# The normaliser's mean as two one-pass products of the squares' halves, split on VectorE

## Chip, cores, metric

One core of a Trainium2 chip. The metric is the device time of one execution in us; the kernel before and each other kernel are run in turns on the same chip, and a ratio is the mean time of one kernel's fast runs over the mean of the other's of the same rounds, so not quite the ratio of the medians that are quoted. The sets of runs were made on different chips, so times of two sets can be compared only roughly: the median of the kernel before lay between 1119.8 and 1122.7 us from set to set. One profiled execution of each kernel gives its trace; a span in a trace is some 2 us shorter than the time of the same execution.

## The reference

```python
def attention(q, k, v, g_norm):            # q, k, v: 8 batches x 8 heads x 576 x 64
    kv  = einsum('bhsd,bhse->bhde', k, v)
    out = einsum('bhsd,bhde->bhse', q, kv)
    rms = sqrt(mean(out * out, axis=-1, keepdims=True) + 1e-06)     # over the 64 of a head
    return out / rms * g_norm

def ffn(x, w_in, w_out):                   # x: 4608 x 512, w_in: 512 x 2048, w_out: 2048 x 512
    h = x @ w_in
    return (h * erf(softplus(h))) @ w_out
```

x is the attention's result, the heads side by side. The weights arrive as 64-bit floats, which the kernel decodes on the chip.

## The kernel before

Work goes by groups of 512 tokens, feature by token: batches 0 to 7, and a ninth group of the 64 tokens left over of each. For a pair of heads the mean over 64 features is a product with a matrix of 1/64, which also spreads the sum over the 64 partitions. Everything is fp32.

```python
def apply():                                   # the output of two heads, and its square
    nc.tensor.matmul(o_ps, lhsT=bd, rhs=qT[:, 0:G], start=True, stop=True)
    ...
    nc.scalar.activation(qT[:, 0:G], o_ps, AF.Square)

def norm():
    ms_ps, u = bank("ms_ps"), st.pop("qT")[:, 0:G]
    nc.tensor.matmul(ms_ps, lhsT=mean_w, rhs=u, start=True, stop=True)      # the mean, 128x512
    nc.scalar.activation(r, ms_ps, AF.Ln, bias=eps_col)                     # r = ms ** -0.5
    nc.scalar.activation(r, r, AF.Exp, scale=-0.5)
    nc.scalar.activation(u, r, AF.Square)
    ... three VectorE steps: one Newton step, times g, into xT ...
```

While one batch goes through the two big products, the attention of the next is done in pieces between them. Batch 0's feed-forward runs in 16 steps of 128 hidden features, beside the decoding of the weights and batch 1's attention:

```python
pieces = attention_pieces(1)               # products, apply, norm for each pair of heads
for n in range(FC):                        # 16 steps
    if n - LAG + 1 >= 0:
        gated(hs[n - LAG + 1], ss[n - LAG + 1])    # VectorE, waits for ScalarE's erf
    if n % BATCH < 3:
        next(pieces)()
    weights(2)                             # join two decoded blocks, split two more
    ... 4 matmuls into h_ps; ScalarE: copy, softplus, every 4th step erf of four units ...
```

From batch 1 on, the two products go block by block with seven multiplications in place of eight (`p_ps` and the sums `a_sums`, `x_sums`, `w_sums`). The first such batch begins with `sums_a`, `sums_x(1)`, then four late gates, then the copy that frees TensorE's bank (one of the buffers that its products go to) for the first product on `x_sums`. From there on a period is one quarter of a batch: 7 + 7 block products and one pair of heads.

Of the kernel before, what the change touches and what calls it, by code (L numbers as in the profile page):

```python
# [37 lines left out]

FP32 = mybir.dt.float32
I32 = mybir.dt.int32  # L40
U32 = mybir.dt.uint32
AF = mybir.ActivationFunctionType
ALU = mybir.AluOpType
# [5 lines left out]
BATCH = 4  # L49
# [4 lines left out]
def kernel(  # L54
# [10 lines left out]
    nc = tc.nc  # L65
    P = 128
    B, H, S, D = q.shape
    DM, DF = moe_w_in.shape[0], moe_w_in.shape[1] // 2
    J = 4
    G = J * P  # L70
    R = S - G
# [8 lines left out]
    const = ctx.enter_context(tc.tile_pool(name="const", bufs=1))  # L80
# [5 lines left out]
    room = ctx.enter_context(ExitStack())  # L86
    early = room.enter_context(tc.tile_pool(name="early", bufs=2))
# [42 lines left out]
    for i in range(2):  # L130
        nc.sync.dma_start(
            out=g_col[i * D : i * D + D, :], in_=g_norm.rearrange("(d one) -> d one", one=1)
# [4 lines left out]

    ident = const.tile([P, P], FP32, name="ident")
    make_identity(nc, ident)
    mean_w = const.tile([P, P], FP32, name="mean_w")  # L140
    nc.vector.memset(mean_w, 0.0)
    for i in range(2):
        nc.vector.memset(mean_w[i * D : i * D + D, i * D : i * D + D], 1.0 / D)
    exp_col = const.tile([P, 1], FP32, name="exp_col")
    nc.vector.memset(exp_col, -896.0 * (1 << 23))
    eps_col = const.tile([P, 1], FP32, name="eps_col")
# [22 lines left out]
    def w_split(which, f):  # L169

        hi = w_raw[which, f].rearrange("p (n two) -> p n two", two=2)[:, :, 1]
        e = early.tile([P, G], I32, name="w_e", tag="w_e", bufs=3)
        m = early.tile([P, G], I32, name="w_m", tag="w_m", bufs=3)
        nc.vector.tensor_scalar(  # L174
            out=e,
            in0=hi,
            scalar1=20,
            scalar2=0x7FF,
            op0=ALU.logical_shift_right,
            op1=ALU.bitwise_and,  # L180
        )
        nc.vector.tensor_scalar(  # L182
            out=e, in0=e, scalar1=896.0, scalar2=1151.0, op0=ALU.max, op1=ALU.min
        )
        nc.scalar.activation(e, e, AF.Identity, scale=float(1 << 23), bias=exp_col)  # L185
        nc.vector.tensor_scalar(  # L186
            out=m,
            in0=hi,
            scalar1=0xFFFFF,
            scalar2=0x100000,  # L190
            op0=ALU.bitwise_and,
            op1=ALU.bitwise_or,
        )
        nc.gpsimd.tensor_scalar(
            out=m.bitcast(FP32), in0=m, scalar1=2.0**-20, scalar2=None, op0=ALU.mult
        )
        w_cv[which, f] = e, m
# [44 lines left out]
    def attention(T, p, pools=None):  # L242

        st = {}
        bd = bd_kv[:, (T * NP + p) % 2, :]

        q_tail, o_tail = slice(P, P + R), slice(P + R, P + 2 * R)
        sb, bufs = (early, 3) if T == 0 else (attp, 1)

        def bank(name):  # L250
            pool, tag = (pools or {}).get(name, (ps_at, "at"))
            return pool.tile([P, G], FP32, name=name, tag=tag)

        def products():
            kv_ps = st["kv"] = bank("kv_ps")
            ks, vs, qs = (x.pop((T, p)) for x in (k_sb, v_sb, q_sb))
            for c in range(C):
                nc.tensor.matmul(  # L258
                    kv_ps[:, 0:P], lhsT=ks[:, c], rhs=vs[:, c], start=(c == 0), stop=(c == C - 1)
                )  # L260
            nc.tensor.transpose(kv_ps[:, q_tail], qs[0:R, J], ident[0:R, 0:R])
            qT = st["qT"] = sb.tile([P, G + R], FP32, name="qT", tag="qT", bufs=bufs)
            for i in range(2):
                s = slice(i * D, i * D + D)
                nc.vector.tensor_copy(out=bd[s, s], in_=kv_ps[s, s])
            nc.vector.tensor_copy(out=qT[:, G:], in_=kv_ps[:, q_tail])
            qt_ps = bank("qt_ps")
            for j in range(J):
                nc.tensor.transpose(qt_ps[:, j * P : j * P + P], qs[:, j], ident)  # L269
            nc.scalar.copy(qT[:, 0:G], qt_ps)  # L270

        def apply():
            qT, o_ps, kv_ps = st["qT"], bank("se_ps"), st.pop("kv")
            nc.tensor.matmul(kv_ps[:, o_tail], lhsT=bd, rhs=qT[:, G:], start=True, stop=True)
            nc.tensor.matmul(o_ps, lhsT=bd, rhs=qT[:, 0:G], start=True, stop=True)  # L275
            nc.vector.tensor_copy(out=x_last[:, p, T * R : T * R + R], in_=kv_ps[:, o_tail])
            st["o"] = o_ps
            nc.scalar.activation(qT[:, 0:G], o_ps, AF.Square)  # L278

        def square():  # L280
            st["o"] = x_last[:, p, :]
            st["qT"] = sb.tile([P, G + R], FP32, name="qT", tag="qT", bufs=bufs)
            nc.scalar.activation(st["qT"][:, 0:G], st["o"], AF.Square)

        def norm():
            ms_ps, u = bank("ms_ps"), st.pop("qT")[:, 0:G]
            nc.tensor.matmul(ms_ps, lhsT=mean_w, rhs=u, start=True, stop=True)  # L287
            r = sb.tile([P, G], FP32, name="rms_r", tag="rms_r", bufs=bufs)
            if T > 0:
                exp_ln_table()  # L290
            nc.scalar.activation(r, ms_ps, AF.Ln, bias=eps_col)
            nc.scalar.activation(r, r, AF.Exp, scale=-0.5)
            nc.scalar.activation(u, r, AF.Square)  # L293
            if T > 0 or p == NP - 1:
                softplus_table()
            nc.vector.scalar_tensor_tensor(  # L296
                out=u, in0=ms_ps, scalar=EPS, in1=u, op0=ALU.add, op1=ALU.mult
            )
            nc.vector.scalar_tensor_tensor(
                out=u, in0=u, scalar=3.0, in1=r, op0=ALU.subtract, op1=ALU.mult  # L300
            )
            if T not in xT:
                xT[T] = xp.tile([P, KC, G], FP32, name="xT", tag="xT")
            nc.vector.scalar_tensor_tensor(
                out=xT[T][:, p, :],
                in0=st.pop("o"),
                scalar=gm_col,
                in1=u,
                op0=ALU.mult,
                op1=ALU.mult,  # L310
            )

        return (products, apply, norm) if T < B else (lambda: None, square, norm)

    def attention_pieces(T):


        for p in range(NP):
            products, apply, norm = attention(T, p)

            def first(products=products, p=p):
                products()
                load_pair(T * NP + p + 2)

            yield from (first, apply, norm)


    NB = FC // BATCH
# [28 lines left out]
    def softplus(h):  # L357
        s = unit("s_sb")
        nc.scalar.activation(s, h, AF.Softplus)  # L359
        return s  # L360
# [22 lines left out]
        for p in range(NP)  # L383
    ]
    for i in range(NP + 2):
        for stage, p in enumerate((i, i - 1, i - 2)):
            if 0 <= p < NP:
                first[p][stage]()
                if stage == 0:
                    if p == 0:  # L390
                        load_pair(3)
                    elif p < 3:
                        load_pair(p + 3)
        if i >= 2:
            weights(1)


    pieces = attention_pieces(1)
    hs, ss = {}, {}
    for n in range(FC):  # L400
        if n - LAG + 1 >= 0:
            gated(hs[n - LAG + 1], ss[n - LAG + 1])

        if n % BATCH < 3:
            next(pieces)()
        weights(2)
        h_ps = ps_h.tile([P, G], FP32, name="h_ps", tag="h")
        for c in range(KC):
            nc.tensor.matmul(  # L409
                h_ps,  # L410
                lhsT=w_in_sb[:, c, n * P : n * P + P],
                rhs=xT[0][:, c, :],
                start=(c == 0),
                stop=(c == KC - 1),
            )
        h = hs[n] = unit("h_sb")
        nc.scalar.copy(h, h_ps)  # L417
        ss[n] = softplus(h)
        if n % BATCH == BATCH - 1:
            erfs([ss[i] for i in range(n - BATCH + 1, n + 1)])  # L420
        if n - LAG >= 0:
            project(n - LAG, hs[n - LAG])

    room.close()
    late = room.enter_context(tc.tile_pool(name="late", bufs=1))
    acc = room.enter_context(tc.tile_pool(name="acc", bufs=6))
    a_sums = late.tile([P, NB, 3, 2, 2 * P], FP32, name="a_sums")
    w_sums = late.tile([P, NB, 3, 2, H], FP32, name="w_sums")

# [131 lines left out]
    def batch(m, before, seconds, slots):  # L561


        T, b = divmod(m, NB)
# [6 lines left out]
        def piece():  # L571
            if todo:
                todo.pop(0)()

        def second():
            for _ in range(next(places)):
                seconds.pop(0)()
# [19 lines left out]
        add(c22, c21, p5)  # L597
        add(c12, c12, p5)
        e22 = softplus(c22)
        second()  # L600
        piece()
        add(c21, c21, product(a22, t4))
# [21 lines left out]
    for m in range(NB, NG * NB):  # L624
        T, b = divmod(m, NB)
# [46 lines left out]
```

## Time and profile before

| | value | read from |
|---|---|---|
| time | 1121.2 us (1119.7 to 1121.7) | 3 runs |
| TensorE busy, 300 us to 900 us | 100%, clock 1.00 | busy time by stage |
| period of that part | 28.26 us in 22 of the 27 intervals between 28 means (the first is 29.93, the last four 25.1 to 25.8) | starts of the means |
| one mean, start to the next product | 0.86 us | timeline |
| VectorE busy, 50 us to 200 us | 76 to 83% | busy time by stage |
| four steps of batch 0's feed-forward | 42.1 us | starts of the gates (VectorE's h times erf) that wait for erf |

How to read it: a timeline line gives start, length, engine, source line, operation, destination and sources, and in square brackets the idle time before it with what ended it. Lengths of matmuls overlap, so prices are taken from one start to the next. The prediction below shows the lines.

### The profile page before, as it was taken

Reading aid. Unit: us, or ns where it says so; the run is one execution under the profiler, and the core shown is the slowest. Engines: PE = TensorE matmul, PEld = TensorE weight load, DVE = VectorE, ACT = ScalarE, POOL = GpSimd, SP = SyncE. Lnnn points to the kernel's source line nnn. Section 1 sums busy time; section 2 is a strip of 40 time slices with the busy share of each in tenths; the row PEclk is TensorE's granted clock in tenths of the full one; section 3 lists DMA queues with packets and bytes.
Section 4 is the critical chain, followed back from the end, with each engine's and each line's share of the span. In section 5 each row is a group of like instructions: output and inputs, shape, how many; then the busy total and the mean of one; then the engine's idle time right before and its main releaser. Section 6 shows DMA issues by size and latency. Waiting matters only on the chain.

```text
span 1121.4 us, 11926 instructions
## 1 busy us (share of the span) xinstructions
PE 1050.5 (94%) x4584; PEld 836.8 (75%) x4584; DVE 713.6 (64%) x1180; ACT 486.5 (43%) x652; POOL 100.7 (9%) x71
## 2 busy tenths in 40 slices
PE   6576887899999999999999999999999999999996
PEld 4232443458888888888888888888888888888885
DVE  1678788637776656675567556755675567666545
ACT  1444444544444444444444444444444455442222
POOL 0257556200000000000000000000000000000000
PEclk9886988999999999999999999999999999999999
DMA  8345434102111211121112111211120001001001
GB/s 206 97 123 146 125 94 127 32 10 61 32 32 32 70 33 32 32 70 32 32 32 70 32 32 32 70 32 33 32 70 1 1 1 38 1 1 38 1 1 38
DMA packets 134488, 55.30 MB, mean 49 GB/s; under 512 B 115488, under 2 KB 131872, under 8 KB 134432
## 3 DMA queue, kind: packets, MB, share of 16 engines
q1 hardware_dynamic: 134432, 54.55, 18.5%
q8 instruction: 36, 0.59, 0.2%
q14 instruction: 20, 0.16, 0.0%
HBM read 45.09 MB, written 9.44 MB: 49 GB/s over the span
## 4 chain that ended last, share of the span: by engine, by line
PE 82%; DVE 10%; ACT 4%; issue 2%; SPq 1%; POOL 0%; DMA 0%; DVEq 0%; ACTq 0%; POOLq 0%
PE p_ps L483 68%; PE kv_ps L258 3%; PE o_ps L336 3%; PE se_ps L275 2%; DVE w_m L207 2%; PE ms_ps L287 2%; DVE e L431 1%; PE qt_ps L269 1%; DVE w_e L203 1%; DVE w_e L182 1%; PE h_ps L409 1%; DVE w_e L174 1%; SPq L121 1%; DVE w_m L186 1%; ACT w_e L185 1%
## 5 line engine op out<-in xcount | busy, mean ns | idle before, releaser
L359 ACT ACTIVATE s_sb<-h_sb 128x512 f32<-128x512 f32 x144 | 89.9, 630 | 337.5 <-DVE h_sb L431 337.0
L431 DVE TENSOR_TENSOR h_sb<-h_sb,p_ps 128x512 f32<-128x512 f32 x224 | 148.2, 684 | 116.0 <-PE p_ps L483 114.8
L483 PE MATMUL p_ps<-w_out_sb,h_sb 128*128 128x256 f32 x768 | 176.4, 380 | 1.0 <-DVE h_sb L585 1.0
L483 PEld LDWEIGHTS p_ps<-w_out_sb,h_sb 128*128 128x128 f32 x768 | 145.8, 190 | 21.5 <-DVE h_sb L585 1.8
L483 PE MATMUL p_ps<-x_sums,a_sums 128*128 128x256 f32 x512 | 122.8, 384 | 4.9 <-issue 4.9
L431 DVE TENSOR_TENSOR e<-e,p_ps 128x512 f32<-128x512 f32 x120 | 80.8, 684 | 71.6 <-PE p_ps L483 71.0
L483 PE MATMUL p_ps<-x_sums,w_in_sb 128*128 128x256 f32 x512 | 121.0, 379 | 0.0
L483 PEld LDWEIGHTS p_ps<-x_sums,a_sums 128*128 128x128 f32 x512 | 98.4, 192 | 28.9 <-issue 16.2
L483 PE MATMUL p_ps<-w_sums,s_sb 128*128 128x256 f32 x512 | 116.3, 380 | 0.0
L483 PEld LDWEIGHTS p_ps<-x_sums,w_in_sb 128*128 128x128 f32 x512 | 97.4, 190 | 25.1 <-issue 13.4
L483 PEld LDWEIGHTS p_ps<-w_sums,s_sb 128*128 128x128 f32 x512 | 95.2, 190 | 15.9 <-DVE h_sb L431 4.0
L483 PE MATMUL p_ps<-xT,w_in_sb 128*128 128x256 f32 x448 | 101.3, 379 | 0.0
L483 PEld LDWEIGHTS p_ps<-xT,w_in_sb 128*128 128x128 f32 x448 | 83.3, 190 | 10.3
L98 ACT ACT_TABLE_LOAD x69 | 88.5, 1283 | 1.2
L431 DVE TENSOR_TENSOR h_sb<-h_sb,s_sb 128x512 f32<-128x512 f32 x128 | 82.2, 685 | 5.5 <-ACT s_sb L364 5.5
L296 DVE SCALAR_TENSOR_TENSOR qT<-ms_ps,qT 128x512 f32<-128x512 f32 x36 | 24.9, 692 | 95.5 <-ACT qT L293 95.5
L409 PE MATMUL h_ps<-xT,w_in_sb 128*128 128x512 f32 x128 | 67.2, 672 | 16.4 <-ACT h_sb L417 11.0
L364 ACT ACTIVATE s_sb<-s_sb 128x512 f32<-128x512 f32 x144 | 78.8, 618 | 0.4
L278 ACT ACTIVATE qT<-se_ps 128x512 f32<-128x512 f32 x32 | 19.0, 594 | 115.5 <-PE se_ps L275 115.5
L409 PEld LDWEIGHTS h_ps<-xT,w_in_sb 128*128 128x128 f32 x128 | 27.8, 221 | 53.6 <-issue 32.6
L258 PEld LDWEIGHTS kv_ps<-v_sb,k_sb 96*128 96x128 f32 x384 | 51.8, 206 | 16.4 <-issue 12.8
L185 ACT ACTIVATE w_e<-w_e,exp_col 128x512 int32<-128x512 int32 x32 | 23.1, 722 | 89.5 <-DVE w_e L182 89.5
(76 smaller groups left out, 1374.7 us busy)
## 6 DMA issues: line engine op xcount, KB each, us to landing
k_sb<-in_k_dram SPq DMA_DIRECT2D x64, 144.0 KB, 3.0
v_sb<-in_v_dram SPq DMA_DIRECT2D x64, 144.0 KB, 3.1
q_sb<-in_q_dram SPq DMA_DIRECT2D x64, 128.0 KB, 2.9
w_raw<-in_moe_w_in_dram SPq DMA_DIRECT2D x16, 512.0 KB, 3.7
w_raw<-in_moe_w_out_dram SPq DMA_DIRECT2D x16, 512.0 KB, 3.8
out_dram<-e SPq DMA_DIRECT2D x28, 256.0 KB, 2.1
q_sb<-in_q_dram SPq DMA_DIRECT2D x32, 32.0 KB, 2.5
out_dram<-o_sb SPq DMA_DIRECT2D x4, 256.0 KB, 2.2
```

Source lines behind the costliest of these rows:

```text
L98: nc.scalar.preload_act_table_set("softplus")
L185: nc.scalar.activation(e, e, AF.Identity, scale=float(1 << 23), bias=exp_col)
L207: nc.vector.scalar_tensor_tensor(out=m, in0=lo, scalar=2.0**-52, in1=m, op0=ALU.mult, op1=ALU.add)
L258: nc.tensor.matmul(kv_ps[:, 0:P], lhsT=ks[:, c], rhs=vs[:, c], start=(c == 0), stop=(c == C - 1))
L275: nc.tensor.matmul(o_ps, lhsT=bd, rhs=qT[:, 0:G], start=True, stop=True)
L296: nc.vector.scalar_tensor_tensor(out=u, in0=ms_ps, scalar=EPS, in1=u, op0=ALU.add, op1=ALU.mult)
L336: nc.tensor.matmul(o_ps[j], lhsT=g[:, j * P : j * P + P], rhs=w_out_sb[:, f, :], start=(f == 0), stop=(f == FC - 1),)
L359: nc.scalar.activation(s, h, AF.Softplus)
L364: nc.scalar.activation(s, s, AF.Erf)
L409: nc.tensor.matmul(h_ps, lhsT=w_in_sb[:, c, n * P : n * P + P], rhs=xT[0][:, c, :], start=(c == 0), stop=(c == KC - 1),)
L431: nc.vector.tensor_tensor(out=out_, in0=x, in1=y, op=op)
L483: nc.tensor.matmul(ps[:, i * H : i * H + H], lhsT=a[:, c, i * P : i * P + P], rhs=x[:, c, :], start=(first and c == 0 and (i == 0 or last) ...
```

## The change

Intent: a product of fp32 operands costs TensorE four passes, one of float32r operands a single pass. The matrix of 1/64 is exact in float32r; the squares are not, so VectorE cuts them in two: the upper half is a copy converted to float32r, the lower half is the square minus it. Two one-pass products into the same bank make the sum.

```diff
+        def halve():
+            u = st.pop("qT")[:, 0:G]
+            hi = st["hi"] = sb.tile([P, G], FP32R, name="sq_hi", tag="rms_r", bufs=bufs)
+            lo = st["lo"] = sb.tile([P, G], FP32R, name="sq_lo", tag="sq_lo", bufs=min(bufs, 2))
+            nc.vector.tensor_copy(out=hi, in_=u)
+            nc.vector.tensor_tensor(out=lo, in0=u, in1=hi.bitcast(FP32), op=ALU.subtract)
 ...
         def norm():
-            ms_ps, u = bank("ms_ps"), st.pop("qT")[:, 0:G]
-            nc.tensor.matmul(ms_ps, lhsT=mean_w, rhs=u, start=True, stop=True)
+            ms_ps = bank("ms_ps")
+            nc.tensor.matmul(ms_ps, lhsT=mean_w, rhs=st.pop("hi"), start=True, stop=False)
+            nc.tensor.matmul(ms_ps, lhsT=mean_w, rhs=st.pop("lo"), start=False, stop=True)
+            u = sb.tile([P, G + R], FP32, name="u", tag="qT", bufs=bufs)[:, 0:G]
 ...
-            yield from (first, apply, norm)
+            yield from (first, apply, halve, norm)
 ...   (batch 0: halve of pair p stands behind norm of pair p-1)
-        if n % BATCH < 3:
-            next(pieces)()
+        next(pieces)()
 ...   (later batches: a fourth place for a piece, before the last two block products)
         e22 = softplus(c22)
+        piece()
         second()
 ...   (room for the lower halves: decoder tiles w_e, w_m 3 -> 2 buffers, accumulators 6 -> 5)
```

More of the change, by code (lines that the diff above doesn't have):

```diff
@@ L39 @@
 FP32 = mybir.dt.float32
+FP32R = mybir.dt.float32r
 I32 = mybir.dt.int32
@@ L139 @@
     make_identity(nc, ident)
-    mean_w = const.tile([P, P], FP32, name="mean_w")
-    nc.vector.memset(mean_w, 0.0)
+    mean_w = const.tile([P, P], FP32R, name="mean_w")
+    mean_f = early.tile([P, P], FP32, name="mean_f", tag="w_e", bufs=2)
+    nc.vector.memset(mean_f, 0.0)
     for i in range(2):
-        nc.vector.memset(mean_w[i * D : i * D + D, i * D : i * D + D], 1.0 / D)
+        nc.vector.memset(mean_f[i * D : i * D + D, i * D : i * D + D], 1.0 / D)
+    nc.vector.tensor_copy(out=mean_w, in_=mean_f)
     exp_col = const.tile([P, 1], FP32, name="exp_col")
@@ L171, in w_split @@
         hi = w_raw[which, f].rearrange("p (n two) -> p n two", two=2)[:, :, 1]
-        e = early.tile([P, G], I32, name="w_e", tag="w_e", bufs=3)
-        m = early.tile([P, G], I32, name="w_m", tag="w_m", bufs=3)
+        e = early.tile([P, G], I32, name="w_e", tag="w_e", bufs=2)
+        m = early.tile([P, G], I32, name="w_m", tag="w_m", bufs=2)
         nc.vector.tensor_scalar(
@@ L311, in norm @@
             )
-        return (products, apply, norm) if T < B else (lambda: None, square, norm)
+        return (products, apply, halve, norm) if T < B else (lambda: None, square, halve, norm)
     def attention_pieces(T):
         for p in range(NP):
-            products, apply, norm = attention(T, p)
+            products, apply, halve, norm = attention(T, p)
             def first(products=products, p=p):
@@ L385 @@
     for i in range(NP + 2):
-        for stage, p in enumerate((i, i - 1, i - 2)):
+        for stage, p in ((0, i), (1, i - 1), (3, i - 2), (2, i - 1)):
             if 0 <= p < NP:
@@ L425 @@
     late = room.enter_context(tc.tile_pool(name="late", bufs=1))
-    acc = room.enter_context(tc.tile_pool(name="acc", bufs=6))
+    acc = room.enter_context(tc.tile_pool(name="acc", bufs=5))
     a_sums = late.tile([P, NB, 3, 2, 2 * P], FP32, name="a_sums")
```

## The prediction

> **What bounds the kernel now.** I read the page first, then the busy time by stage, then the instructions that touch the mean's tile ms_ps, then the timeline of one steady period and of the two stages before it. From the page (engine busy shares, and the chain that ended last):
>
> ```profile
> PE 1050.5 (94%) x4584; PEld 836.8 (75%) x4584; DVE 713.6 (64%) x1180; ACT 486.5 (43%) x652; POOL 100.7 (9%) x71
> ...
> PE 82%; DVE 10%; ACT 4%; issue 2%; SPq 1%; POOL 0%; DMA 0%; DVEq 0%; ACTq 0%; POOLq 0%
> ```
>
> TensorE is the bound, but not everywhere: 10% of the chain is VectorE. The stages say where (columns: stretch in us, its length, busy us of TensorE, weight loads, VectorE, ScalarE, GpSimd with instruction counts, granted clock, DMA share, GB/s):
>
> ```profile
> 50.00:100.00 50.00, 27.66 (x61) 11.94 (x59) 37.87 (x60) 23.80 (x35) 28.94 (x19) 0.76 0.46 130
> 100.00:150.00 50.00, 41.62 (x99) 19.16 (x99) 41.61 (x64) 24.52 (x35) 30.65 (x20) 0.86 0.43 123
> ...
> 300.00:400.00 100.00, 100.00 (x485) 85.79 (x484) 70.81 (x120) 48.65 (x65) 0.00 (x0) 1.00 0.17 43
> ```
>
> So there are two kernels in one. Up to about 210 us (loading, decoding the weights from 64-bit floats, the attention of batches 0 and 1) the three elementwise engines hand work round and VectorE sets the pace. From about 235 us TensorE is busy 100% at full clock, with VectorE at 60 to 71%. What a shorter matmul saves is real only in the second; what VectorE is given costs only in the first.
>
> The mean's product in the steady part, with its neighbours (start us, length us, engine, line):
>
> ```profile
> 437.94 1.89 PE L483 MATMUL p_ps<-w_out_sb,h_sb 128*128 128x256 f32 x8
> 439.66 1.02 PE L287 MATMUL ms_ps<-qT,mean_w 128*128 128x512 f32 x2
> ...
> 440.52 1.89 PE L483 MATMUL p_ps<-x_sums,w_in_sb 128*128 128x256 f32 x8
> ```
>
> Starts, not lengths, give the cost, since lengths overlap: 440.52 - 439.66 = 0.86 us for one fp32 mean, recorded as 2 instructions. All 36 means are 72 records.
>
> **What the Trainium skill says.** "FP8 and Floating Point Precision", TensorE Precision Notes: true fp32 takes 4 passes through the array, and a reduced-precision fp32 reads 4 bytes and truncates to a 22-bit format. "TensorE: Matmul & The Clock Gate", Back-to-back issue gap: a warm pass costs N/2.4 + 2.5 ns, 216 ns for 512 columns. Four of these are 0.864 us: the trace's 0.86 agrees, so the mean now pays four passes. That a float32r product is one pass of that length is in the change's description; no line here shows it yet. "VectorE: DVE Perf Modes", The perf-mode tier table: a copy or scalar op on fp32 in SBUF reaches 2x, a tensor-tensor op only 1x. The trace agrees: single-input ops of 128x512 take 0.41 to 0.42 us, tensor-tensor ones 0.68 to 0.69. "TensorE: Matmul & The Clock Gate", What's actually happening: after an idle window of about 3.4 us the clock falls to half; this matters at one place below, where the trace shows a clock of 0.50.
>
> **Removed on TensorE.** 36 times one four-pass product, and in its place two one-pass ones over the same 512 columns: 2 x 216 = 0.43 us instead of 0.86. The weight loads lie under the previous matmul either way. Of the 36, batches 0 and 1 (8 means) fall in the stage that TensorE does not set. Batches 2 to 8, 28 means, one per period of 28.26 us, fall where it is the bound. Saving: 28 x 0.43 = 12.0 us.
>
> **Added on VectorE.** 36 copies (fp32 to float32r, the upper half) and 36 subtractions (the lower half). Working from its rows: a dependent single-input op costs 0.45 us start to start (33.20 to 33.65 in batch 0), a tensor-tensor op followed by independent work 0.60. I take 1.1 us a pair if the copy keeps the 2x rate, 1.35 if the conversion loses it; 39 to 49 us of busy time in all, 64% becoming 68 to 69%.
>
> - Steady part, hidden. In the period shown, the additions that precede the new piece end at 437.7. The pair ends by about 438.9, and TensorE reaches the mean only at 439.66, after two more products. VectorE stood idle 2.17 us just then, until 439.86. So TensorE should not wait, with 0.7 us to spare.
> - Batch 0, partly on the path. The pair of heads p is placed behind the normalisation of p-1. Behind it come weight decoding, ScalarE's decoding step, and, in ScalarE's order, the next logarithm, so a delay on VectorE goes round. The first pair lies in idle time and the shorter cold product gives back about 0.6 us; three more cost 1.1 each: 3.3 - 0.6 = +2.7.
> - Batch 1, on the path. A four-step cycle takes 42.1 us. I add a pair to each of three cycles: 3 x 1.1 = +3.3. The wait for ScalarE's square (4.37 us) moves by one step with the normalisation and stays.
>
> **Moved, and here I expect the unplanned gain.** The pieces of batch 1 are now four in four steps, so its last normalisation stands in the last step instead of the one before. VectorE before:
>
> ```profile
> 198.76 0.68 DVE L368 TENSOR_TENSOR h_sb<-h_sb,s_sb 128x512 f32<-128x512 f32 x1
> 203.81 0.69 DVE L296 SCALAR_TENSOR_TENSOR qT<-ms_ps,qT 128x512 f32<-128x512 f32 x1 [4.37 <-ACT qT L293]
> ...
> 205.94 0.68 DVE L203 SCALAR_TENSOR_TENSOR w_e<-w_raw,w_e 128x512 int32<-128x512 int32 x1
> ...
> 211.26 0.69 DVE L431 TENSOR_TENSOR a_sums<-w_in_sb 128x512 f32<-128x512 f32 x1 [1.17 <-POOL w_out_sb L216]
> ```
>
> It waits 4.37 us for ScalarE, and then joins the last weights, 3.5 us. In the changed order the pair and the joins come first, while ScalarE makes the square. In old time: gate to 199.4, pair to 200.7, joins to 204.2, gate to 204.9. ScalarE, without the old order's wait, copies the next step (200.5 to 201.7), loads its table, and ends the square near 205.1; the three steps of normalisation end at 207.3, so the sums start there and not at 211.26: 4 us earlier. TensorE waits for exactly these:
>
> ```profile
> 220.50 3.75 PE L483 MATMUL p_ps<-x_sums,a_sums 128*128 128x256 f32 x8 [4.86 <-issue]
> ...
> 220.50:224.00 3.50, 3.50 (x8) 2.83 (x9) 0.69 (x1) 0.63 (x1) 0.00 (x0) 0.50 0.02 5
> 224.00:232.50 8.50, 8.50 (x20) 3.80 (x19) 0.69 (x1) 0.00 (x0) 0.00 (x0) 0.85 0.00 0
> ```
>
> The view calls the 4.86 us "issue", but VectorE's list up to 220.4 is the bank that this product needs. The wait shrinks to about 1 us: -4.0. After it the clock is 0.50, and 8 products take 3.5 us against 1.73 in the steady part, and 16 take 8.1 against 6.87. With a wait below the idle window that loss of about 3.1 us should largely vanish; I count 0.7 of it, -2.2.
>
> **Buffers.** The decoder's e and m go from three buffers to two: the second split then waits for GpSimd's product of the second join. In the trace that ends at 112.64 and the split starts at 113.18; elsewhere 126.79 and 127.33. Half a microsecond free: cost 0. One accumulator less (6 to 5) meets stores that land in about 2 us, some 8 us before the buffer is wanted: 0.
>
> Sum: -12.0 + 2.7 + 3.3 - 4.0 - 2.2 = -12.2; 1121.2 - 12.2 = 1109.0 us.
>
> **Rivals.**
> 1. A float32r pass is not one column per cycle (twice that, or a stall at a change of type). For: nothing in this trace has the type. Against: two-pass fp32 records fit one column per cycle per pass. It would leave 0.86 for the two, remove the 12.0 and end near 1121.
> 2. TensorE waits for the halves in the steady part, an engine of 64% becoming a bound in places. For: only 0.7 us of slack, and the strict order on VectorE. Against: the idle 2.17 us there. If it waited the 0.4 it saves, again about 1121; at 0.2, near 1115.
> 3. The ramp pays more: VectorE runs beside GpSimd (the clamp takes 1.37 us beside GpSimd's product, 0.43 alone), and two buffers lock the three engines. Doubling each pair in the ramp and losing the reordering gain would give 1121.2 - 12.0 + 12 = 1121.
> 4. The reorder gains nothing because GpSimd or TensorE ends later than I drew: 1115.
>
> **Range and chances.** The firm term is 12.0; the ramp's terms nearly cancel, each uncertain by 2 to 4. Hence 1102 to 1117 for 8 in 10, wider above than below because three rivals point there. Faster by 2% means below 1098.8: all 36 means saved (15.5) plus the whole transition (7) and a free ramp, 4%. Slower by 2% means 1143.6, beyond every rival added singly: 2%. Within: 94%.
>
> **What would show it.** Means in the steady part 0.43 us start to start, a period of 27.83 us for 28.26; TensorE still 100% from 300 us; no new wait of TensorE for the halves; copy 0.42 and subtraction 0.69 us, VectorE about 68% busy; the first product on x_sums after a wait of about 1 us at a clock well above 0.50; the first 200 us later by about 6. A mean of 0.86, a period still 28.2, or a ramp longer by over 10 us would prove me wrong.

## The result

| | before | changed |
|---|---|---|
| median of 4 runs | 1121.45 us (1119.7 to 1122.9) | 1109.46 us (1108.8 to 1111.8) |
| ratio of the fast runs | | 0.9897 (0.9877 to 0.9918) |
| span of the profiled execution | 1121.4 us | 1107.4 us |

A second set of four runs, below, gave 1109.18 us and a ratio of 0.9888. The gain is inside the 2% to which the prediction gave 94%. The two traces differ by 14.0 us, the mean times by 11.5; the difference is scatter between executions (the profiled one of the kernel before took 1123.18 us, above its three other runs), which is taken up below.

The page after: the same TensorE share, more VectorE, nearly the same split of the chain.

```profile
PE 1036.5 (94%) x4584; PEld 837.0 (76%) x4584; DVE 750.9 (68%) x1253; ACT 486.2 (44%) x652; POOL 100.5 (9%) x71
...
PE 81%; DVE 11%; ACT 4%; issue 2%; SPq 1%; DMA 0%; POOL 0%; DVEq 0%; ACTq 0%; POOLq 0%
```

TensorE lost 14.0 us of busy time and VectorE gained 37.3. The number of TensorE records is the same, because an fp32 product was recorded as two as well.

The steady part after, TensorE, its weight loads and VectorE around one mean:

```profile
431.66 0.42 DVE L287 CAST sq_hi<-qT 128x512 fp32r<-128x512 f32 x1
...
431.98 1.89 PE L494 MATMUL p_ps<-w_out_sb,h_sb 128*128 128x256 f32 x8
432.11 0.69 DVE L288 TENSOR_TENSOR sq_lo<-qT,sq_hi 128x512 fp32r<-128x512 f32 x1
433.49 0.19 PEld L298 LDWEIGHTS ms_ps<-sq_hi,mean_w 128*128 128x128 f32 x1
433.52 0.59 PE L298 MATMUL ms_ps<-sq_hi,mean_w 128*128 128x512 f32 x1
433.71 0.19 PEld L299 LDWEIGHTS ms_ps<-sq_lo,mean_w 128*128 128x128 f32 x1
433.91 0.69 DVE L442 TENSOR_TENSOR e<-e,p_ps 128x512 f32<-128x512 f32 x1 [1.10 <-PE p_ps L494]
433.94 0.40 PE L299 MATMUL ms_ps<-sq_lo,mean_w 128*128 128x512 f32 x1
...
434.18 1.89 PE L494 MATMUL p_ps<-x_sums,w_in_sb 128*128 128x256 f32 x8
```

The cast runs at 0.42 us and the subtraction at 0.69, and both are over 0.7 us before TensorE asks for them; VectorE still idles 1.10 us afterwards, where it idled 2.17. From the last product before the mean to the first after it: 434.18 - 431.98 = 2.20 us, before it was 440.52 - 437.94 = 2.58. So a mean saves 0.38 us there, and the period falls from 28.263 to 27.875 us, 0.39, not the 0.43 that the passes alone would give. The records start early here (the first product's at 433.52, while the eight records before it, 0.216 us from start to start, last until 433.71), so the reader should take the sum and not the start of the first product.

The end of batch 1's attention after, VectorE and then TensorE with the stages around the first product on x_sums:

```profile
202.57 0.68 DVE L381 TENSOR_TENSOR h_sb<-h_sb,s_sb 128x512 f32<-128x512 f32 x1
203.17 0.41 DVE L287 CAST sq_hi<-qT 128x512 fp32r<-128x512 f32 x1
203.62 0.98 DVE L288 TENSOR_TENSOR sq_lo<-qT,sq_hi 128x512 fp32r<-128x512 f32 x1
...
206.33 1.76 DVE L210 SCALAR_TENSOR_TENSOR w_m<-w_raw,w_m 128x512 f32<-128x512 uint32 x1
...
208.76 0.69 DVE L309 SCALAR_TENSOR_TENSOR u<-ms_ps,u 128x512 f32<-128x512 f32 x1
...
211.07 0.68 DVE L442 TENSOR_TENSOR a_sums<-w_in_sb 128x512 f32<-128x512 f32 x1
```

```profile
220.29 1.97 PE L494 MATMUL p_ps<-x_sums,a_sums 128*128 128x256 f32 x8 [2.68 <-issue]
222.09 7.03 PE L349 MATMUL o_ps<-w_out_sb,h_sb 128*128 128x512 f32 x16
228.96 0.33 PE L277 MATMUL kv_ps<-qT,bd_kv 128*128 128x64 f32 x2
```

```profile
220.29:223.79 3.50, 3.50 (x12) 2.36 (x13) 1.37 (x2) 0.63 (x1) 0.00 (x0) 1.00 0.16 35
```

VectorE no longer waits 4.37 us for ScalarE between the gate and the normalisation: the halves and the joins fill that time. The product still starts at 220.29, hardly earlier than 220.50 before, because everything ahead of it had become later. But the clock behind it is 1.00 instead of 0.50, and 8 + 16 records take 8.67 us (220.29 to 228.96) instead of 11.68 (220.50 to 232.18).

Where the 14.0 us between the traces went, by landmarks of the two timelines:

| stretch | before | changed | difference |
|---|---|---|---|
| start to the last normalisation step of batch 0 | 55.33 | 56.40 | +1.1 |
| from there to the gate of step 12 | 127.16 | 129.89 | +2.7 |
| from there to the first product on x_sums | 38.01 | 34.00 | -4.0 |
| 24 records behind it | 11.68 | 8.67 | -3.0 |
| from there to the end (28 means) | 889.2 | 878.4 | -10.8 |

### The profile page after: what moved, and what is told of

It is laid out like the page before. It is cut to its first block, busy times and chain, and to the rows that moved or that the text cites. A ratio compares the mean times of both kernels' runs of the same rounds, so it can differ in the third digit from the quotient of the medians.

```text
span 1107.4 us, 11999 instructions
## 1 busy us (share of the span) xinstructions
PE 1036.5 (94%) x4584; PEld 837.0 (76%) x4584; DVE 750.9 (68%) x1253; ACT 486.2 (44%) x652; POOL 100.5 (9%) x71
## 4 chain that ended last, share of the span: by engine, by line
PE 81%; DVE 11%; ACT 4%; issue 2%; SPq 1%; DMA 0%; POOL 0%; DVEq 0%; ACTq 0%; POOLq 0%
PE p_ps L494 69%; PE kv_ps L261 3%; DVE w_m L210 3%; PE o_ps L349 2%; PE se_ps L278 2%; DVE e L442 1%; DVE w_e L206 1%; PE qt_ps L272 1%; DVE w_e L185 1%; PE h_ps L420 1%; DVE w_e L177 1%; SPq L122 1%; DVE w_m L189 1%; PE ms_ps L299 1%; PE ms_ps L298 1%
## 5 line engine op out<-in xcount | busy, mean ns | idle before, releaser
L261 PE MATMUL kv_ps<-v_sb,k_sb 96*128 96x128 f32 x384 | 56.2, 303 | 23.3 <-DVE u L309 13.3
L309 DVE SCALAR_TENSOR_TENSOR u<-ms_ps,u 128x512 f32<-128x512 f32 x36 | 24.9, 691 | 77.5 <-ACT u L306 77.5
L261 PEld LDWEIGHTS kv_ps<-v_sb,k_sb 96*128 96x128 f32 x384 | 54.8, 217 | 29.8 <-DVE u L309 15.8
```

The source lines that it names most:

```text
L261: nc.tensor.matmul(kv_ps[:, 0:P], lhsT=ks[:, c], rhs=vs[:, c], start=(c == 0), stop=(c == C - 1))
L309: nc.vector.scalar_tensor_tensor(out=u, in0=ms_ps, scalar=EPS, in1=u, op0=ALU.add, op1=ALU.mult)
```

## The experiments

The theory: four terms add up. (1) TensorE's passes, about 0.39 us for each of 28 means. (2) VectorE's pairs cost only in the first 200 us. (3) The normalisation's new place at the end of batch 1 gives back 4 us. (4) The shorter wait there keeps the clock up, another 3 us. The rivals: the order has no part in it and the passes are all; the pairs also cost in the steady part; the loss in the ramp (the first 220 us) is the smaller buffers'. All kernels gave results that passed the comparison with the reference, also the one that was wrong; how exact the halves are was not measured.

The landmarks of every trace (us; "cycle" is half the time between the gates of steps 4 and 12; "wait" is TensorE's, right before the first product on x_sums; "+24" the time of the 24 records behind that product):

| run | batch 0 done | cycle | wait | product on x_sums | +24 | period | median time | ratio |
|---|---|---|---|---|---|---|---|---|
| before | 55.33 | 42.08 | 4.86 | 220.50 | 11.68 | 28.263 | 1121.45 | 1 |
| changed | 56.40 | 43.00 | 2.68 | 220.29 | 8.67 | 27.875 | 1109.46 | 0.9897 |
| order alone | 55.87 | 42.06 | 0.98 | 217.47 | 8.67 | 28.266 | 1116.66 | 0.9947 |
| halves unread | 56.35 | 43.00 | 2.38 | 220.24 | 8.66 | 28.267 | 1120.78 | 0.9994 |
| old step | 58.24 | 42.08 | 0 | 226.34 | 8.59 | 27.871 | 1114.24 | 0.9930 |
| upper half alone | 55.69 | 42.42 | 2.77 | 217.62 | 8.67 | 27.635 | 1099.33 | 0.9807 |
| small buffers | 55.19 | 42.07 | 3.40 | 220.60 | 11.43 | 28.264 | 1120.16 | 0.9997 |
| filler | 54.10 | 42.08 | 0 | 219.99 | 8.59 | 28.265 | 1119.34 | 0.9984 |
| late halves | 53.85 | 42.07 | 2.16 | 215.06 | 8.67 | 27.867 | 1104.86 | 0.9849 |
| gates later | 55.25 | 42.06 | 0 | 217.15 | 8.59 | 27.869 | 1102.76 | 0.9827 |
| changed, again | 57.85 | 43.00 | 0.98 | 221.88 | 8.67 | 27.872 | 1109.18 | 0.9888 |
| old step thrice | 57.88 | 42.10 | 1.04 | 219.34 | 8.67 | 27.867 | 1107.29 | 0.9867 |
| late halves, again | 53.42 | 42.08 | 0.97 | 215.16 | 8.67 | 27.871 | 1104.33 | 0.9867 |
| gates later, again | 54.07 | 42.08 | 0 | 212.99 | 8.60 | 27.867 | 1103.17 | 0.9849 |

**1. The order alone.** The kernel before, four places for pieces in place of three:

```diff
-            yield from (first, apply, norm)
+            yield from (first, apply, lambda: None, norm)
-        if n % BATCH < 3:
-            next(pieces)()
+        next(pieces)()
         e22 = softplus(c22)
+        piece()
         second()
```

> The fp32 mean of the kernel before, with nothing halved; only the place of the pieces is new (four slots, so the last normalisation of batch 1 stands one step later and behind the last weight joins). Theory: the reordering alone is worth 4 us at the first product on x_sums and about 3 us more because TensorE's clock no longer falls to 0.50 there: 1113 to 1115.5 us, wait before that product 1 to 2.5 us instead of 4.86, clock above 0.9 after it, steady period still 28.26 us. Rival (all of the gain is the one-pass product): 1120 to 1122, wait and clock as before.

Measured 1116.66 us, ratio 0.9947 (0.9932 to 0.9962): faster by 5.5 us in the means, a little less than expected (the median lies 1.2 us above the range). From the gate of step 12 to the first product on x_sums it takes 34.46 us instead of 38.01, and 8.67 instead of 11.68 behind it. The wait, in the order-alone kernel:

```profile
217.47 1.96 PE L482 MATMUL p_ps<-x_sums,a_sums 128*128 128x256 f32 x8 [0.98 <-issue]
219.27 7.03 PE L336 MATMUL o_ps<-w_out_sb,h_sb 128*128 128x512 f32 x16
```

The period is 28.27, as before: no mean has become cheaper. So 5.5 us, where the whole change gained 11.5, need no float32r at all. The rival that the order plays no part falls.

**2. The halves made and read by nobody.** The changed kernel, whose mean is the fp32 product of the squares again:

```diff
-            nc.tensor.matmul(ms_ps, lhsT=mean_w, rhs=st.pop("hi"), start=True, stop=False)
-            nc.tensor.matmul(ms_ps, lhsT=mean_w, rhs=st.pop("lo"), start=False, stop=True)
+            nc.tensor.matmul(ms_ps, lhsT=mean_w, rhs=u, start=True, stop=True)
 ...   (mean_w is fp32 again, and the square is kept for the mean)
```

> The changed kernel with the halves still made on VectorE but read by nobody; the mean is the fp32 product of before. Theory: it loses exactly the products' saving, 28 periods x 0.39 = 10.9 us, against the changed kernel: 1118 to 1121 us, steady period 28.26 us, TensorE still 100% busy, so VectorE's 36 pairs cost the steady part nothing; against the order-only kernel it is 3 to 5 us slower, all before 200 us. Rival (VectorE's pairs also delay the steady part): a period above 28.3, over 1122.

Measured 1120.78 us, ratio 0.9994. Against the order alone it is 4.1 us slower in the medians and 5.0 in the means; both have the same steady period to 0.001 us, so the pairs cost the steady part nothing. The two traces differ by only 2.7 us, and all of that lies before the first product on x_sums (220.24 against 217.47). Against the changed kernel it is 11.3 us slower, near the 28 x 0.39 = 10.9 of the passes. As expected.

**3. The old steps.** The changed kernel, with batch 1's normalisation back in the third of four steps, its pair directly ahead of it:

```diff
-        next(pieces)()
+        for _ in range((1, 1, 2, 0)[n % BATCH]):
+            next(pieces)()
```

> The changed kernel with batch 1's pieces at the steps they had before (halves and normalisation both in the third of four steps). Theory: the 4 us and the clock's 3 us are lost again: 1115 to 1118 us, first product on x_sums at 224 to 226 us after a wait of 4 to 6 us, clock 0.5 to 0.6 in the 3.5 us after it, steady period 27.88. Rival (the order does not matter): 1109 to 1111.

Measured 1114.24 us, below the range: slower than the changed kernel by 4.8 in the medians, 3.7 by the ratios, near what the order should be worth, but not in the way I wrote. TensorE's timeline and one stage of the old-step kernel:

```profile
203.00 0.80 PE L298 MATMUL ms_ps<-sq_hi,mean_w 128*128 128x512 f32 x1 [4.28 <-DVE sq_hi L287]
204.02 0.80 PE L299 MATMUL ms_ps<-sq_lo,mean_w 128*128 128x512 f32 x1 [0.22 <-DVE sq_lo L288]
204.61 6.01 PE L421 MATMUL h_ps<-xT,w_in_sb 128*128 128x512 f32 x8
...
226.34 1.03 PE L495 MATMUL p_ps<-x_sums,a_sums 128*128 128x256 f32 x4
```

```profile
203.00:210.00 7.00, 6.78 (x9) 3.00 (x10) 3.91 (x6) 5.14 (x6) 1.29 (x1) 0.54 0.00 0
```

The product on x_sums came where I expected it (226.34), but after no wait, at a clock of 1.00. The wait had moved forward to the mean itself: TensorE stands 4.28 us until VectorE has the upper half, and the clock's loss follows that wait (0.54; 8 records in 5.85 us, to 210.46). The fp32 mean needs only ScalarE's square, and in the kernel before it ran at 195.30, ahead of the gate at 198.76; here the cast stands behind the gate (201.93) in VectorE's order, and the mean with it. The two earlier such means of batch 1 wait for the upper half as well (3.15 us at 118.83 and 4.17 at 160.91); in the changed kernel no mean after 76 us waits for its halves. The second surprise is the cycle: 42.08 us with the pairs in it, exactly that of before, where the changed kernel has 43.00. VectorE of the same kernel shows why:

```profile
159.84 0.68 DVE L381 TENSOR_TENSOR h_sb<-h_sb,s_sb 128x512 f32<-128x512 f32 x1
160.44 0.41 DVE L287 CAST sq_hi<-qT 128x512 fp32r<-128x512 f32 x1
160.89 0.98 DVE L288 TENSOR_TENSOR sq_lo<-qT,sq_hi 128x512 fp32r<-128x512 f32 x1
164.89 0.69 DVE L309 SCALAR_TENSOR_TENSOR u<-ms_ps,u 128x512 f32<-128x512 f32 x1 [3.02 <-ACT u L306]
```

The pair lies in the 4.37 us that VectorE waits for ScalarE anyway, of which 3.02 are left.

**4. The upper half alone**, wrong: one float32r product, no subtraction.

```diff
-            nc.vector.tensor_tensor(out=lo, in0=u, in1=hi.bitcast(FP32), op=ALU.subtract)
 ...   (the tile of the lower half goes too)
-            nc.tensor.matmul(ms_ps, lhsT=mean_w, rhs=st.pop("hi"), start=True, stop=False)
-            nc.tensor.matmul(ms_ps, lhsT=mean_w, rhs=st.pop("lo"), start=False, stop=True)
+            nc.tensor.matmul(ms_ps, lhsT=mean_w, rhs=st.pop("hi"), start=True, stop=True)
```

> Wrong on purpose: the mean of the upper halves alone, one product and no subtraction; the result loses bits of the squares. It prices one float32r product. Theory: a product of 512 columns costs one column per cycle, so the steady period falls by 0.21 to 0.25 us to about 27.65 (28 x 0.22 = 6 us), and the ramp loses about 0.65 us for each of 7 subtractions on its path, less 1 to 2 hidden: 1100 to 1103.5 us. Rival (the first float32r product of a pair costs the most, for the change of type): the period stays above 27.75.

Measured 1099.33 us, ratio 0.9807; a little faster than the range. The period is 27.635: the second product costs 27.875 - 27.635 = 0.24 us. The first then costs 0.86 - (28.263 - 27.635) = 0.23. No extra cost of the first, for a change of type, shows; both cost a little more than 0.216, a quarter of the fp32 mean's 0.86. Its trace:

```profile
427.66 1.89 PE L491 MATMUL p_ps<-w_out_sb,h_sb 128*128 128x256 f32 x8
429.20 0.58 PE L296 MATMUL ms_ps<-sq_hi,mean_w 128*128 128x512 f32 x1
429.62 1.89 PE L491 MATMUL p_ps<-x_sums,w_in_sb 128*128 128x256 f32 x8
```

429.62 - 427.66 = 1.96, 0.23 more than the 1.73 of the eight records. In the ramp the cycle is 42.42, so of the pair's 0.92 us the cast is 0.34 and the subtraction 0.58.

**5. The smaller buffers alone**, in the kernel before.

```diff
-        e = early.tile([P, G], I32, name="w_e", tag="w_e", bufs=3)
-        m = early.tile([P, G], I32, name="w_m", tag="w_m", bufs=3)
+        e = early.tile([P, G], I32, name="w_e", tag="w_e", bufs=2)
+        m = early.tile([P, G], I32, name="w_m", tag="w_m", bufs=2)
-    acc = room.enter_context(tc.tile_pool(name="acc", bufs=6))
+    acc = room.enter_context(tc.tile_pool(name="acc", bufs=5))
```

> The kernel before with the changed kernel's buffers only: e and m of the decoder two deep, five accumulators. Theory: GpSimd's product ends about 0.5 us before the buffer is wanted, so nothing changes: 1120 to 1122.5 us, the four-step cycle of the ramp still 42.1 us. Rival (the three engines lock together): 2 to 10 us slower, with new waits of VectorE for GpSimd ahead of the first decoding step.

Measured 1120.16 us, ratio 0.9997 (0.9979 to 1.0015), cycle 42.07. The buffers cost nothing; that rival falls. Its wait ahead of the product on x_sums was 3.40 us in this trace, and the clock was 0.50 there.

**6. Filler in the wait.** The kernel before, with ten products that nobody reads where TensorE waits 4.86 us:

```diff
-            qt_ps = bank("qt_ps")
+            qt_ps = spare[0] = bank("qt_ps")      # an attention bank, free by then
 ...
+        if m == NB:
+            for _ in range(10):
+                nc.tensor.matmul(
+                    spare[0][:, 0 : 2 * P], lhsT=ident, rhs=w_out_sb[:, 0, 0:H], start=True, stop=True
+                )
         add(c12, c12, product(s2, t2))
```

> The kernel before with ten fp32 products of 128x256 that nobody reads put into TensorE's 4.86 us wait before the first product on x_sums (4.3 us of work, on a bank that is free). Theory: the wait's cost is twofold, and the second part is the clock: the product on x_sums still starts at 220.5, but 8 records then take about 1.8 us instead of 3.5 and the next 16 about 6.9 instead of 8.1, so 1117.5 to 1119.5 us, 2.5 to 3.5 below before. Rival (the clock falls for another reason or later work absorbs it): 1121 to 1122.

In the trace of the filler kernel:

```profile
215.67 4.48 PE L593 MATMUL qt_ps<-w_out_sb,ident 128*128 128x256 f32 x20
219.99 1.89 PE L484 MATMUL p_ps<-x_sums,a_sums 128*128 128x256 f32 x8
221.71 7.03 PE L337 MATMUL o_ps<-w_out_sb,h_sb 128*128 128x512 f32 x16
228.58 0.33 PE L275 MATMUL kv_ps<-qT,bd_kv 128*128 128x64 f32 x2
```

8.59 us for the 24 records instead of 11.68: 3.1 us from the clock alone, by doing useless work. In time: 1119.34 us, inside the range, but only 1.7 us below the mean of before, and the interval (0.9968 to 1.0001) just reaches 1. The reason is in the runs of before. In this set five of its eleven lay between 1118.3 and 1119.9 us (mean clock 0.973 to 0.976) and six between 1121.1 and 1123.4 (0.969 to 0.973); the filler's six all lay between 1117.9 and 1120.1. It looks as if not every execution of before loses the clock at that place; the low runs left no trace that could show it.

**7. Halves only from batch 2 on.** Where TensorE is not the bound, the mean stays fp32:

```diff
         def halve():
+            if T < 2:
+                return
 ...
+            if T < 2:
+                u = st.pop("qT")[:, 0:G]
+                nc.tensor.matmul(ms_ps, lhsT=mean_f, rhs=u, start=True, stop=True)
+            else:
+                ... as in the changed kernel ...
 ...   (the fp32 matrix mean_f gets a buffer of its own)
```

> The changed kernel with the halves only from batch 2 on; batches 0 and 1, where TensorE is not the bound, keep the fp32 mean and no VectorE work is added. Theory: the ramp's cost of about 3.8 us goes, the steady saving stays: 1104.5 to 1107 us, first product on x_sums 3 to 5 us earlier than in the changed kernel, period 27.88. Rival (the ramp's cost was the smaller decoder buffers or chance, not the pairs): 1109 to 1110.5.

Measured 1104.86 us, ratio 0.9849 (0.9832 to 0.9866), as expected: cycle 42.07, batch 0 done at 53.85, product on x_sums at 215.06 (5.2 us earlier, where 3 to 5 were expected), period 27.867. No run of this kernel reached the fastest of the changed one's (1103.9 to 1106.3 against 1108.8 to 1111.8). It was run again beside run 12:

> The kernel with halves only from batch 2 on, again, beside the next on the same chip. Theory: 1103.5 to 1106.5 us as before.

1104.33 us median of five (1104.3 to 1107.3), mean 1105.4.

**8. The four late gates behind the bank's copy**, on top of 7:

```diff
-    before = (last_gates, lambda: None, lambda: None)
+    before = (lambda: None, last_gates, lambda: None)
```

> The kernel with halves only from batch 2 on, and the four gates of the first part's last units put behind the copy that frees TensorE's bank instead of ahead of it. Theory: the 2.16 us that TensorE still waits before the first product on x_sums is VectorE's list in order, 2.4 us of it these gates; the wait goes below 0.3 us and the time falls by about 2: 1102 to 1104 us. Rival (the sums of x themselves end that late, or the gates are then missed by the projections): 1104.5 to 1106.

Measured 1102.76 us (1101.3 to 1106.2). The profiled execution was one of the slow ones, and it shows one source of this kernel's scatter: at another place the clock was down, and TensorE came to the product on x_sums late, with no wait left to see. TensorE and the stage in it:

```profile
188.00 5.70 PE L425 MATMUL h_ps<-xT,w_in_sb 128*128 128x512 f32 x8
...
188.00:193.50 5.50, 5.50 (x9) 2.26 (x8) 5.47 (x10) 3.03 (x5) 4.29 (x4) 0.62 0.30 95
```

These 8 records took 5.54 us; in run 7's trace the same took 3.43. So I ran 7 and 8 once more on one chip:

> The same with the four gates behind the bank's copy, again. Its first five runs lay at 1101.3 to 1102.8 (three) and 1106.1 to 1106.2 (two); the profiled one was of the latter and had no wait before the first product on x_sums, but a late TensorE. Theory: at the first product on x_sums a wait below 0.3 us, and a mean 1 to 2.5 us below the other kernel's. Rival (the gates' place gives nothing, the three low runs were chance): means within 0.7 us of each other.

Median 1103.17 us of four, mean 1103.6 against 1105.4 for the other, ratios to before 0.9849 (0.9826 to 0.9871) and 0.9867 (0.9846 to 0.9889). The trace of the second run has no wait:

```profile
209.53 3.62 PE L499 MATMUL p_ps<-xT,w_in_sb 128*128 128x256 f32 x16
212.99 1.89 PE L499 MATMUL p_ps<-x_sums,a_sums 128*128 128x256 f32 x8
```

The wait is gone, as the theory has it. In time the gain over 7 is 1.8 us in these means and inside the overlap of the intervals, so its size is not settled. Both kernels beat the changed one and the one before: all their 18 runs lie at or below 1107.3, all eight of the changed kernel's at or above 1108.8.

**9. The changed kernel again**, for its scatter:

> The changed kernel unaltered, again, for its scatter beside the kernel before's. The kernel before ran at 1118.3 to 1119.9 us with a mean clock of 0.973 to 0.976 or at 1121.1 to 1123.4 with 0.969 to 0.973. Theory: the upper group is the executions in which the clock falls after the 4.86 us wait; the changed kernel's wait is 2.68 us, so most of its runs should lie in one group: 1108.5 to 1110.5, at most one or two of six above 1111. Rival (the two groups have another cause): as many of them 2.5 to 3.5 us above the others as in the kernel before.

1109.18 us; three of four between 1108.9 and 1109.4, one at 1111.46. The first four were alike (1108.8 to 1109.6, and one at 1111.79). So it has a slower group too, two of its eight runs, against 22 of 31 of before's in the first three sets of experiments and 4 of 9 in the fourth. Its profiled slow execution had no low clock behind the product on x_sums (1.00); batch 0 was done 1.45 us later than in the first trace, at 57.85. So the scatter has more than one cause: batch 0's start, the place at 188 us in run 8, and the wait of before. The rival is right in part.

What decides at such a place can be counted in the traces. Their record of the granted clock holds only 1.00 and 0.50, and in all fourteen it changes only at steps of a fixed grid of 3.413 us (212 stretches, each a multiple of it to 0.002 us); the 0.62 and 0.85 of the stages above are averages. I took each piece of that grid from 100 to 250 us that was at 1.00, 524 in all: all 33 with TensorE busy for at most 42% were followed by 0.50, none of the 466 above 61% was, and 9 of the 25 between were. So a wait of 2 to 3 us can cost the clock or not, by how it falls on the grid: the changed kernel's 2.68 us was split over two pieces that were 68% and 53% busy, in run 8's trace the wait of 2.53 us left one 13% busy. The 4.86 us of before left one piece (216.34 to 219.75) with no work, and wherever such a wait falls, one piece is at most 29% busy (an estimate: half the wait, 2.43, out of 3.41). If the low runs of before kept the clock there, their wait was shorter; that stays open.

**10. The first three pairs in the old step**, the last normalisation in its new one:

```diff
-        next(pieces)()
+        for _ in range((1, 1, 2, 0)[n % BATCH] if n < FC - BATCH else 1):
+            next(pieces)()
```

> The changed kernel with batch 1's first three pairs in the old step, ahead of the wait for ScalarE, and only the last normalisation in its new step. Theory: in the run with the old steps the four-step cycle was 42.08 us with the pairs in it, as in the kernel before, because they lie in VectorE's 4.37 us wait; so the changed kernel's 43.0 falls to 42.08 three times, 2.8 us, while the 4 us at the end of batch 1 stay: 1106 to 1107.5. Rival (the old steps are bad throughout): 1109.5 or more.

Measured 1107.29 us, ratio 0.9867: 2.4 us below the changed kernel of the same set in the means, cycle 42.10. Where VectorE waits anyway, the pair is free; a step later it is not.

## Why the prediction was right, by its own steps

The time, 1109.46 us, lies on the predicted 1109.0; this owes something to errors that cancel, so each term:

| term | predicted | shown |
|---|---|---|
| passes, 28 means | -12.0 | -10.8 in the traces, 0.385 a mean |
| pairs in batch 0 | +2.7 | +1.1 in the first trace; 57.3 against 54.6 us over five traces with and eight without, each group within 2.5 us: +2.7 |
| pairs in batch 1, three cycles | +3.3 | +2.7, 3 x 0.92 |
| normalisation's new place | -4.0 | -4.0 (34.00 for 38.01); -3.6 by the order alone |
| clock behind the wait | -2.2 | -3.0 in the traces; in time less, since before does not seem to lose it in each execution |
| pairs in the steady part | 0 | 0 (period equal to 0.001 us) |
| buffers | 0 | 0 (ratio 0.9997) |

**The bound** was read rightly: two stages with different limits, and the pairs cost only in the first, the passes pay only in the second. Runs 2 and 7 show both halves of that separately. That VectorE's wait of 4.37 us moves by one step and stays came true as well (at 173.53 in the changed kernel); that the old step's wait could have hidden the pair was not seen, and run 10 shows it.

**The step that was mis-sized** is "2 x 216 = 0.43 us instead of 0.86. The weight loads lie under the previous matmul either way." A float32r product of 512 columns costs 0.23 to 0.24 us, a pair 0.47. The trace suggests why: the load of the matrix takes 0.19 us, as for fp32, and in the timeline after the change the second product starts (433.94) just as its load ends (433.90), and the load behind it starts then (433.95). A pass of 0.216 is nearly as short as a load with its gaps. No run took the load away, so this cause is argued and not shown. The 28 equal periods of the prediction were not quite so either: 22 intervals save 0.39 us, the last four 0.33 to 0.40, the first 0.18.

**The wait** was predicted at about 1 us and was 2.68: the sums came 4.0 us earlier against the gate, as drawn, but TensorE itself reached that point 1.8 us earlier against the same gate (31.3 us for 33.2), so more of the wait was left. That nothing was lost is in part luck: the wait fell across two pieces of the clock's grid. Within one piece it would have left that piece 21% busy (an estimate, (3.41 - 2.68) / 3.41), and all pieces counted with so little work lost the clock.

**Rival 1** (no one-pass rate) falls with the period. **Rival 2** (TensorE waits for the halves) holds nowhere in the changed kernel's steady part, but outside it, at the end of batch 1, it is what happened in run 3: the order that the change chose is what keeps it away there. **Rival 3** (a dearer ramp) holds in one line of the trace, the subtraction beside GpSimd at 0.98 us for 0.69, but the second join that follows is quicker in turn (0.60 us to its next, 1.02 at the same place in the order-alone kernel, where GpSimd's scaling still runs beside it); the net was 0.92, below my 1.1. **Rival 4** falls with run 1.

## What to carry to other kernels

Ask of every added instruction in which stage it falls, and of every saved one too: here the same edit paid 10.8 us in one stage and cost some 5 in the other, and doing it only where it pays was worth another 4.6 to 4.9 us in the medians of the sets, 2 to 5 by their ratios. When a change also moves work, measure the move alone; 5.5 of the 11.5 us came with the new order alone. And put a new step where its engine waits anyway: one step later it cost 0.92 us each time.

## What the Trainium skill lacked or had wrong

- "FP8 and Floating Point Precision", TensorE Precision Notes: it names the reduced form of fp32 but gives no cost. Here a float32r product of 128x512 took 0.23 to 0.24 us, a four-pass one 0.86.
- "TensorE: Matmul & The Clock Gate", LDWEIGHTS (loading the stationary operand): its formula, columns over 1.2, gives 107 ns for 128 columns; the loads of fp32 and float32r matrices here took 0.19 us, at a clock of 1.00. Back-to-back issue gap gives N/2.4 + 2.5 ns for the isolated product, 0.02 us too short for the one-pass products of 512 columns here, and about 131 ns in a stream of loads and products, where these took 0.23 to 0.24 us.
- The same page, What's actually happening: it lets the clock fall to half after one idle window of about 3.4 us that runs freely. The grid of 3.413 us and the half clock agree, but the window need not be idle: pieces in which TensorE was busy for up to 42% all lost the clock (33 of 33), pieces above 61% never (0 of 466). The page gives no such share.
- "VectorE: DVE Perf Modes", The perf-mode tier table: float32r as a destination is not in it; the cast from fp32 ran at 0.42 us, the rate of the fp32 single-input operations.
